# An attention-plus-maxout kernel on one core: subs of eight chunks, the linear term in one phase, evictions over several banks, a fixed order

## The chip, the cores and the metric

The kernel runs on one core of a Trainium2 chip. The metric is the device time of one launch in microseconds, the median of three runs. TensorE (PE in the profile) multiplies and writes to PSUM, which has eight banks of 128 partitions by 512 float32 columns. ScalarE (ACT) and VectorE (DVE) read PSUM and write to SBUF; this is called an eviction here. GpSimd (POOL) and SyncE (SP) mostly issue transfers.

## The reference, cut to what matters

`x` is 4 batches of 12,544 tokens of 128 numbers. Per batch, 32 inducing vectors attend over the tokens and give `h` (32 x 128); each token then attends over `h`. The 50,176 results go through a layer that takes the greater of two products of width 1,024, and a last product back to 128.

```python
def mab(q, kv):                       # softmax attention, scale = 1/sqrt(128)
    s = scale * (q @ kv.transpose(0, 2, 1))
    a = np.exp(s - s.max(-1, keepdims=True))
    a /= a.sum(-1, keepdims=True) + 1e-09
    return a @ kv
h = mab(inducing, x)                  # per batch: 32 x 128
y = mab(x, h).reshape(50176, 128)
g = np.maximum(y @ w1, y @ w2)        # 50176 x 1024
out = g @ w_out                       # 50176 x 128
```

Before and after use `max(a, b) = a + relu(b - a)`. With `e` the 32 exponentials of a token, `b - a` is `e @ hwd` with `hwd = h (w2 - w1)`, and `a @ w_out` is `e @ m1` with `m1 = h w1 w_out`. So a token's output is `(relu(e @ hwd) @ w_out + e @ m1) / sum(e)`. The second term is the **linear term**.

## The kernel before

A chunk is 128 tokens; a batch has 98 chunks, and there are 392. Because `e` has 32 rows, four products `e @ hwd` can run at once, each in its own 32 rows of TensorE's array (row tiles). The kernel therefore has four quarters `q`, each with its own chunks. A **stage** computes `e` of up to 16 chunks in four column tiles (128 x 32) and takes the exponential on ScalarE. A **phase** is a run of row-tile matmuls (32 x 128): each quarter fills one PSUM bank of 512 columns, which ScalarE or VectorE evicts with a relu.

```python
for i in range(4):                       # phase(): the four quarters side by side
    for seq in parts_:
        if i < len(seq):
            nc.tensor.matmul(**seq[i])   # 1 of 512 columns, or 2 of 256, or 4 of 128
...
if max(ck.act, ready) + 0.477 <= max(ck.dve, ready) + 0.597:
    nc.scalar.activation(out=dst, in_=src, func=AF.Relu)      # one bank
else:
    nc.vector.tensor_scalar(out=dst, in0=src, scalar1=0.0, scalar2=None, op0=ALU.max)
```

A **final** is one full-array matmul (128 x 128, 128 columns) that multiplies the relu of one chunk and one eighth of the width by `w_out`; a chunk has eight, so there are 3,136. Finals add up in the bank of their group, which is up to four chunks of one quarter. That bank was opened by the linear term of the group, which took the place of one quarter's unit in a phase; a few groups at the ends take the linear term with full-array matmuls instead.

```python
if kind == "L":                          # a group's linear term in place of a unit
    for s, (_, t) in enumerate(a.chunks):
        seq.append(dict(out=ps[:, 128 * s : 128 * (s + 1)],
                        lhsT=a.blk.e2[r, 128 * t : 128 * (t + 1)],
                        rhs=st[qu.b]["m1"][r, :], start=(s == 0), stop=False, ...))
...
nc.tensor.matmul(                        # final_one()
    out=g.ps[:, 128 * c : 128 * (c + 1)],
    lhsT=g.blk.relu[q][:, 128 * (jb * w4 + t) : 128 * (jb * w4 + t + 1)],
    rhs=woutp[:, jb, :], start=(g.full and state["mm"] == 0), ...)
...
nc.vector.tensor_mul(osb[:, 0:n, :], g.ps[...], rp)   # evict_group(): times 1 / sum(e)
nc.sync.dma_start(out=outr[b, :, c : c + m, :], in_=osb[:, s : s + m, :])
```

What comes next is chosen while the program is built. A class `Clock` keeps an estimate of when each engine and bank is free, and a loop takes a phase, a final, a stage or a part of the next batch's first attention. Where the estimate shows TensorE without work, `keep_busy` puts in matmuls of zeros.

```python
while state["g"] < len(groups) or held:
    side_work()
    ...
    if tp < INF and lag() <= 128 + LIMIT and (tp <= ck.pe + early or tp <= tf and tf > ck.pe):
        phase(jobs)
    elif tf < INF:
        keep_busy(tf)
        final_one()
```

The next batch's attention over its tokens (L309 to L370 in the profile: scores, transposes by DMA, sums in column tiles) is interleaved with the current batch's phases and finals.

Of the kernel before, what the change touches and what calls it, by code (L numbers as in the profile page):

```python
# [16 lines left out]
INF = 1e9  # L17

# [42 lines left out]
class Quarter:  # L61


    def __init__(self, b, c0, w):
        self.b, self.c0, self.w = b, c0, w
        self.subs = {1: [1], 2: [2], 3: [2, 1], 4: [4]}[w]


class Block:


    def __init__(self, quarters, full=()):
        self.quarters = quarters
        self.width = max(qu.w for qu in quarters if qu)
        self.b = [qu.b for qu in quarters if qu][0]
        self.staged = None
        self.rp = None
        self.units = []
        self.done = {}
        self.relu = {}  # L80
        self.last_group = {}
        self.groups = []
        for q, qu in enumerate(quarters):
            jobs = []
            t0 = 0
            for w in qu.subs if qu else []:
                for u in range(2 * w):
                    jobs.append((q, t0, w, u))
                t0 += w
            self.units.append(jobs)  # L90
            if qu:
                self.groups.append(Group(self, [(q, t) for t in range(qu.w)], q in full))


class Group:
    def __init__(self, blk, chunks, full):
        self.blk, self.chunks, self.full = blk, chunks, full
        self.q = chunks[0][0]
        self.bank = self.ps = None
# [3 lines left out]
def kernel(  # L103
# [17 lines left out]
    P1 = 14  # L121
    DOWN = 2.0**-14
    NE2 = 5
    WARM = 9
# [16 lines left out]

    def bank(shape, dtype=F32, only=None):
        i = min(range(8), key=lambda j: ck.bank[j]) if only is None else only
        uid[0] += 1
        return i, psum.tile(shape, dtype, name=f"ps{uid[0]}", tag=f"bank{i}", bufs=1)
# [38 lines left out]
    w2h = relup.tile([128, 4096], F16, name="w2h", tag="relu0")[:, 0:J]  # L184
    w1h = relup.tile([128, 4096], F16, name="w1h", tag="relu1")[:, 0:J]
# [5 lines left out]
    m1bd = consts.tile([128, 4, C], F16, name="m1bd")  # L191
# [5 lines left out]
    with tc.manual_schedule(engines={ET.PE, ET.DVE, ET.Activation, ET.Pool, ET.SP}):  # L197

        xf = relup.tile([128, 4096], F16, name="xf", tag="relu2")[:, 0 : 256 * P1].bitcast(F32)
# [17 lines left out]
        for q in range(4):  # L217
            nc.vector.memset(ones_q[32 * q : 32 * (q + 1), q : q + 1], 1.0)
        nc.gpsimd.memset(m1bd, 0.0)
# [216 lines left out]
        def small_sums(es, ready):  # L436

            ps = st[0]["eps"]
            ck.wait(ready, "p1")
            nc.tensor.matmul(out=ps[:, 2:3], lhsT=rep32, rhs=es, start=True, stop=True, skip_group_check=True)  # L440
            end = ck.run(0.11)
            st[0]["rs"] = smp.tile([128, 1], F32, name="rs_0", tag="rs_")
            st[0]["rw"] = smp.tile([128, 1], F32, name="rw_0", tag="rw_")
            nc.vector.reciprocal(out=st[0]["rs"], in_=ps[:, 2:3])
            nc.vector.tensor_scalar(out=st[0]["rw"], in0=st[0]["rs"], scalar1=1.0 / scale, scalar2=None, op0=ALU.mult)
            ck.bank[st[0]["eb"]] = st[0]["rsr"] = ck.on_dve(end, 0.34)

        def small_hwd(b, halves=(0, 1)):
            if 0 in halves:
                st[b]["hwd"] = smp.tile([128, J], F16, name=f"hwd_{b}", tag="hwd")  # L450
            hwd = st[b]["hwd"]
            for half in halves:
                for n in range(2 if b == 0 and half == 0 else 1):
                    w = 256 if b == 0 and half == 0 else 512
                    bi, ps = bank([128, 512])
                    ps = ps[:, 0:w]
                    sl = slice(512 * half + w * n, 512 * half + w * (n + 1))
                    ck.wait(max(ck.bank[bi], st[b]["hT4r"]), "p1")
                    if b == 0:
                        nc.tensor.matmul(out=ps, lhsT=st[b]["hT4"], rhs=w2h[:, sl], start=True, stop=False)  # L460
                        nc.tensor.matmul(out=ps, lhsT=st[b]["hT4"], rhs=w1h[:, sl], start=False, stop=True)
                        end = ck.run(0.43 * w / 512)
                    else:
                        nc.tensor.matmul(out=ps, lhsT=st[b]["hT4"], rhs=w21[:, sl], start=True, stop=True)  # L464
                        end = ck.run(0.215)
                    if half == 0 and n == 0:
                        if b == 0:
                            nc.vector.tensor_scalar(
                                out=hwd[:, sl], in0=ps, scalar1=st[0]["rw"], scalar2=None, op0=ALU.mult
                            )  # L470
                        else:
                            nc.vector.tensor_copy(out=hwd[:, sl], in_=ps)
                        ck.bank[bi] = ck.on_dve(end, 0.07 + w / 970.0)
                    else:
                        nc.scalar.activation(
                            out=hwd[:, sl], in_=ps, func=AF.Copy, scale=st[0]["rw"] if b == 0 else 1.0
                        )
                        ck.bank[bi] = ck.on_act(end, 0.06 + w / 1200.0)
                    st[b]["hwdr"] = max(ck.bank[bi], st[b].get("hwdr", 0.0))

        def small_m1(b):
# [5 lines left out]
            bd = {0: [0], B - 1: [0, 1, 2, 3]}.get(b, [])  # L487
            outs = [(m1bd[32 * q : 32 * (q + 1), q, :], slice(32 * q, 32 * (q + 1))) for q in bd]
            for o, r in outs + [(m1, slice(0, 128))]:
                if b == 0:  # L490
                    nc.vector.tensor_scalar(
                        out=o, in0=ps[r, 0:128], scalar1=st[0]["rw"][r, :], scalar2=None, op0=ALU.mult
                    )
                else:
                    nc.vector.tensor_copy(out=o, in_=ps[r, 0:128])
                ck.bank[bi] = ck.on_dve(end, 0.2)
# [18 lines left out]
        def weights_2():  # L515
            for g in range(2):
                bi, ps = bank([128, 4, 128], F16)
                ck.wait(ck.bank[bi], "w")
                for j in range(4):
                    jb = 4 * g + j  # L520
                    nc.tensor.transpose(ps[:, j, :], w1h[:, 128 * jb : 128 * (jb + 1)], identity16)
                end = ck.run(0.056 * 4)
                if g == 0:
                    nc.vector.tensor_copy(out=w1T[:, 0:4, :], in_=ps)
                    ck.bank[bi] = ck.on_dve(end, 0.4)
                else:
                    nc.scalar.copy(out=w1T[:, 4:8, :], in_=ps)
                    ck.bank[bi] = w_of["w1T"] = ck.on_act(end, 0.5)

        def weights_3():  # L530
# [15 lines left out]
        def shapes(b):  # L546

            four = [(4, 4, 4, 4)]
            if b == 0:
                return [(1, 2, 3, 4)] + four * 5 + [(2, 2, 2, 2)]  # L550
            if b == 1:
                return four * 6 + [(1, 1, 0, 0)]
            if b == 2:
                return four * 6 + [(0, 0, 1, 1)]
            return four * 5 + [(2, 2, 2, 2), (4, 3, 2, 1)]

        blocks = []
        for b in range(B):
            c0 = 0
            for shape in shapes(b):  # L560
                quarters = []
                for w in shape:
                    quarters.append(Quarter(b, c0, w) if w else None)
                    c0 += w
                blocks.append(Block(quarters, (0,) if not blocks else (0, 1, 2, 3) if shape == (4, 3, 2, 1) else ()))
            assert c0 == K

        def stage(blk):
            bi, ps = bank([128, 512])
            wd = blk.width  # L570
            some = [qu for qu in blk.quarters if qu]
            ck.wait(max(ck.bank[bi], st[some[0].b]["hT4r"]), "stage bank")
            for q in range(4):
                qu = blk.quarters[q] or some[0]
                hq = st[qu.b]["hT4"][:, 32 * q : 32 * (q + 1)]
                xT = xT_tiles[qu.b % 2]
                lo = qu.c0 if qu.c0 + wd <= K else K - wd
                pieces = [(0, qu.c0, min(wd, K - qu.c0))]
                if pieces[0][2] < wd:
                    pieces.append((pieces[0][2], lo, wd - pieces[0][2]))  # L580
                for t, c, n in pieces:
                    nc.tensor.matmul(  # L582
                        out=ps[32 * q : 32 * (q + 1), 128 * t : 128 * (t + n)],
                        lhsT=hq,
# [576 lines left out]
```

The softmax here doesn't subtract the row's maximum and nothing guards it: scores larger than these inputs give would overflow.

## Time and profile before

| | before |
|---|---|
| median of 3 runs | 330.41 us (330.19 to 330.61) |
| span of the profiled execution | 328.5 us |
| busy: TensorE, VectorE, ScalarE | 98%, 87%, 85% of the span |
| mean granted TensorE clock | 1.00 |
| finals (L792), row-tile matmuls of phases (L957) | 3,136 and 1,261 |
| relu evictions: ScalarE (L973), VectorE (L976) | 463 and 321, one bank each |
| evictions of results (L819) | 108 |

Matmuls overlap in the pipeline, so the busy time of a TensorE line counts a stretch once even if several are in flight, and the mean of one (220 ns for a final) is a latency and not what it adds to the time. What one adds is the distance from start to start. For ScalarE and VectorE the mean also overlaps a little with the next instruction. "x" is a count; idle time is that of the engine just before the group, with what ended most of it.

### The profile page before, as it was taken

What the parts mean: (1) busy time and instruction counts of PE and PEld (TensorE: products, weight loads), DVE (VectorE), ACT (ScalarE), POOL (GpSimd) and SP (SyncE); (2) the same over time, 40 slices, a digit from 0 to 9 for tenths busy, and PEclk for the clock granted to TensorE, in tenths of its full rate; (3) what the DMA queues carried; (4) which work ended last, traced back from release to release, by engine and by line L of the source; (5) the groups of instructions that cost most, each with busy time, mean ns of one, the idle gap of its engine ahead of it and who ended that gap; (6) DMA issues with size and microseconds to landing.
All of it is one profiled execution on the core that took longest, in us unless ns stands there. A gap on an engine that the chain in (4) does not pass through costs nothing.

```text
span 328.5 us, 12601 instructions
## 1 busy us (share of the span) xinstructions
PE 322.6 (98%) x5401; PEld 244.1 (74%) x5401; DVE 285.3 (87%) x532; ACT 280.7 (85%) x562; POOL 25.7 (8%) x54
## 2 busy tenths in 40 slices
PE   8999999999999999999999999999999999999996
PEld 3876777777777777777777777777777777778785
DVE  3359899999988999998989989988989989989873
ACT  3679899998789999988888999998968999999961
POOL 7351030000310000000040000000000000000000
PEclk9999999999999999999999999999999999999999
DMA  8999999964299999672479999983212312222233
GB/s 207 208 206 213 289 237 205 216 187 124 57 227 244 229 221 213 167 155 97 132 139 245 226 257 215 197 177 100 98 66 97 114 67 99 98 98 98 80 116 114
DMA packets 70823, 53.65 MB, mean 163 GB/s; under 512 B 52176, under 2 KB 55408, under 8 KB 70768
## 3 DMA queue, kind: packets, MB, share of 16 engines
q1 hardware_dynamic: 64656, 38.63, 47.4%
q0 software_dynamic: 6112, 14.22, 22.1%
q8 instruction: 42, 0.69, 0.9%
q14 instruction: 13, 0.11, 0.1%
HBM read 28.33 MB, written 25.69 MB: 164 GB/s over the span
## 4 chain that ended last, share of the span: by engine, by line
PE 96%; DVE 1%; issue 1%; ACT 0%; DVEq 0%; ACTq 0%
PE ps L792 60%; PE ps L957 22%; PE ps L582 3%; PE ps L232 2%; PE ps L357 1%; PE ps L309 1%; PE ps L648 1%; PE ps L248 1%; PE ps L280 1%; PE ps L622 1%; DVE relu L976 1%; PE ps L749 1%; PE ps L271 1%; PE ps L640 0%; PE ps L464 0%
## 5 line engine op out<-in xcount | busy, mean ns | idle before, releaser
L973 ACT ACTIVATE relu<-ps 128x512 f16<-128x512 f32 x463 | 244.6, 604 | 31.1 <-PE ps L957 24.1
L976 DVE TENSOR_SCALAR relu<-ps 128x512 f16<-128x512 f32 x321 | 205.8, 681 | 18.8 <-PE ps L957 17.9
L792 PE MATMUL ps<-woutp,relu 128*128 128x128 f16 x3136 | 218.1, 220 | 0.0
L792 PEld LDWEIGHTS <-relu 128*128 128x128 f16 x3136 | 177.3, 98 | 39.4 <-issue 28.3
L957 PE MATMUL ps<-e,hwd 32*128 32x512 f16 (+2 forms) x880 | 89.0, 360 | 0.0
L819 DVE TENSOR_TENSOR o<-ps,rp 128x512 f32<-128x512 f32 (+3 forms) x108 | 68.6, 635 | 5.7 <-PE ps L792 3.1
L957 PEld LDWEIGHTS <-hwd 32*128 32x128 f16 x880 | 25.0, 91 | 21.1 <-issue 0.8
L957 PE MATMUL ps<-m,e 32*128 32x128 f16 x381 | 38.8, 217 | 0.0
L957 PEld LDWEIGHTS <-e 32*128 32x128 f16 x381 | 21.4, 92 | 2.6
L165 POOL DMA_DIRECT2D xn<-in_x_dram x31 | 16.7, 551 | 8.4 <-DMA xn<-in_x_dram 4.4
L236 DVE COPY xT<-ps 128x512 f16<-128x512 f16 (+3 forms) x11 | 5.5, 504 | 8.1 <-PE ps L232 8.0
L594 ACT ACTIVATE e<-ps 128x512 f16<-128x512 f32 (+2 forms) x21 | 11.6, 572 | 0.0
L320 ACT ACTIVATE eu<-ps 128x512 f16<-128x512 f32 x18 | 10.8, 619 | 0.0
L582 PE MATMUL ps<-xT,hT 128*32 128x512 f16 (+3 forms) x114 | 10.4, 366 | 0.0
L164 POOL COPY pace<-esr 128x1 f32<-128x1 f32 x2 | 0.4, 183 | 116.6 <-DVE esr L391 116.6
L239 ACT COPY xT<-ps 128x768 f16<-128x768 f16 (+3 forms) x11 | 6.1, 557 | 3.0 <-PE ps L232 2.9
L232 PE MATMUL ps<-identity,xn 128*128 128x128 f16 x98 | 7.7, 224 | 0.1
L582 PEld LDWEIGHTS <-hT 128*32 128x32 f16 x114 | 2.9, 93 | 5.9 <-issue 5.2
L232 PEld LDWEIGHTS <-xn 128*128 128x128 f16 x98 | 5.9, 100 | 1.3 <-DVE xn L644 0.9
L257 ACT ACTIVATE et<-ps 128x448 f16<-128x448 f32 (+4 forms) x11 | 4.5, 413 | 2.6 <-PE ps L248 2.6
L632 DVE RECIPROCAL rp<-ps 128x16 f32<-128x16 f32 (+2 forms) x28 | 6.7, 239 | 0.0
L622 PE MATMUL ps<-ones_q,e 128*128 128x4 f16 x102 | 6.5, 165 | 0.0
(96 smaller groups left out, 117.5 us busy)
## 6 DMA issues: line engine op xcount, KB each, us to landing
out_dram<-o SPq DMA_DIRECT2D x90, 256.0 KB, 2.5
xn<-in_x_dram POOLq DMA_DIRECT2D x24, 448.0 KB, 11.9
out_dram<-o SPq DMA_DIRECT2D x10, 128.0 KB, 3.1
xn<-in_moe_w_dram POOLq DMA_DIRECT2D x4, 256.0 KB, 14.1
xn<-in_x_dram POOLq DMA_DIRECT2D x4, 224.0 KB, 10.2
xT<-xn SPq DMA_TRANSPOSE x42, 3.8
xf<-in_x_dram SPq DMA_DIRECT2D x1, 512.0 KB, 3.7
xf<-in_x_dram SPq DMA_DIRECT2D x1, 384.0 KB, 4.1
```

What stands on the lines that cost most here:

```text
L165: nc.gpsimd.dma_start(out=xn_at[b, i][:, 0:n, :], in_=xr[b, :, k0 : k0 + n, :])
L232: nc.tensor.transpose(ps[:, j, :], xn[:, g + j, :], identity16)
L320: nc.scalar.activation(out=eu, in_=ps, func=AF.Exp, scale=scale, accum_out=st[b]["es"][:, u : u + 1])
L582: nc.tensor.matmul(out=ps[32 * q : 32 * (q + 1), 128 * t : 128 * (t + n)], lhsT=hq, rhs=xT[:, c : c + n, :], start=True, stop=True, tile_p ...
L594: nc.scalar.activation(out=blk.e2[:, 0 : 128 * wd], in_=ps[:, 0 : 128 * wd], func=AF.Exp, scale=st[0]["rs"] if blk.b == 0 else scale,)
L622: nc.tensor.matmul(out=ps[:, 4 * t : 4 * t + 4], lhsT=blk.e2[:, 128 * t : 128 * (t + 1)], rhs=ones_q, start=True, stop=True,)
L632: nc.vector.reciprocal(out=blk.rp[:, 0:wd, :].rearrange("p t q -> p (t q)"), in_=ps[:, 0 : 4 * wd])
L792: nc.tensor.matmul(out=g.ps[:, 128 * c : 128 * (c + 1)], lhsT=g.blk.relu[q][:, 128 * (jb * w4 + t) : 128 * (jb * w4 + t + 1)], rhs=woutp[: ...
L819: nc.vector.tensor_mul(osb[:, 0:n, :], g.ps[:, 0 : n * C].rearrange("p (s c) -> p s c", s=n), rp)
L957: nc.tensor.matmul(**seq[i])
L973: nc.scalar.activation(out=dst, in_=src, func=AF.Relu)
L976: nc.vector.tensor_scalar(out=dst, in0=src, scalar1=0.0, scalar2=None, op0=ALU.max)
```

## The change

A **sub** is now eight chunks in token order, two for each quarter, and there are 49. Every sub has exactly four phases; in each, every quarter makes two eighths of the width for its two chunks, as two matmuls of 256 columns. Quarters 0 and 2 belong to result bank `a`, quarters 1 and 3 to bank `b`, and each of these two banks takes four chunks and 32 finals. The linear term of all eight chunks of a sub rides in one phase of a later sub, as two further matmuls of 128 columns per quarter. Two quarters then write to the same result bank from different row tiles. Quarters 0 and 1 do their linear part first and quarters 2 and 3 last, and a semaphore makes the latter wait until the former have been written.

All of PSUM is one tile, so one relu instruction can read two or three adjacent banks. Which engine evicts which banks, which banks are used, and the order of everything in the main part stand in a list, `ORDER`, that is part of the source; the loop, its readiness rules and `keep_busy` are gone. In that list `PA2D1A1:426L` is a phase whose banks start at 4, 2 and 6: ScalarE takes two, VectorE one, ScalarE one, and the L adds a linear term; `a8` and `b6` are finals.

The aims are phases that are all alike and fewer in number, fewer instructions on the evicting engines, and an order that was fixed beforehand.

```diff
-        def phase(jobs):
-            free = sorted(range(8), key=lambda j: ck.bank[j])
...
-                if kind == "L":
-                    qu = a.blk.quarters[q]
-                    for s, (_, t) in enumerate(a.chunks):
...
-            for i in range(4):
-                for seq in parts_:
-                    if i < len(seq):
-                        nc.tensor.matmul(**seq[i])
+        def phase(segs, banks, linear):
...
+            for i, (q, b) in enumerate(zip((0, 2, 1, 3), units)):
+                seqs[q] = [
+                    dict(
+                        out=ps_all[:, b, 256 * jj : 256 * (jj + 1)],
+                        lhsT=st[sub.at[q][0]]["hwd"][r, 128 * (2 * p + jj) : 128 * (2 * p + jj + 1)],
+                        rhs=sub.tile.e2[r, 256 * sub.slot : 256 * (sub.slot + 1)],
...
+                    for jj in range(2)
+                ]
+            if linear:
...
+                ln = linear_of(ls)
+                for q in range(4):
+                    seqs[q] = ln[q] + seqs[q] if q < 2 else seqs[q] + ln[q]
+            for i in range(len(seqs[0])):
+                for q, seq in enumerate(seqs):
+                    if linear and (i, q) == (2, 2):
+
+                        nc.tensor.wait_ge(apart, at["linear"])
+                    nc.tensor.matmul(**seq[i])
+                    if linear and (i, q) == (1, 1):
+                        at["linear"] += 1
+                        nc.tensor.drain(fusable=True).then_inc(apart, 1)
...
+                dst = sub.relu.rearrange("p (i x) -> p i x", i=4)[:, i : i + w, 512 * p : 512 * (p + 1)]
+                src = ps_all[:, b : b + w, :]
+                if e == "A":
                     nc.scalar.activation(out=dst, in_=src, func=AF.Relu)
                 else:
                     nc.vector.tensor_scalar(out=dst, in0=src, scalar1=0.0, scalar2=None, op0=ALU.max)
...
-        while state["g"] < len(groups) or held:
-            side_work()
...
-                keep_busy(tf)
...
+        run(ORDER)
```

In the built program the drain is no instruction of its own: the matmul of quarter 1 raises the semaphore when it is done, and the weight load of quarter 2's first linear matmul waits for it. Smaller parts of the change: the full-array linear matmuls and their block-diagonal `m1bd` are gone, the weights' transposes go through one bank and one VectorE copy, and the staging buffers follow the subs.

## Prediction

> **What bounds the kernel now.** I read the page's busy shares first, then the chain that ended last, then the costliest groups:
>
> ```profile
> PE 322.6 (98%) x5401; PEld 244.1 (74%) x5401; DVE 285.3 (87%) x532; ACT 280.7 (85%) x562; POOL 25.7 (8%) x54
> ...
> PE 96%; DVE 1%; issue 1%; ACT 0%; DVEq 0%; ACTq 0%
> ...
> L973 ACT ACTIVATE relu<-ps 128x512 f16<-128x512 f32 x463 | 244.6, 604 | 31.1 <-PE ps L957 24.1
> L976 DVE TENSOR_SCALAR relu<-ps 128x512 f16<-128x512 f32 x321 | 205.8, 681 | 18.8 <-PE ps L957 17.9
> L792 PE MATMUL ps<-woutp,relu 128*128 128x128 f16 x3136 | 218.1, 220 | 0.0
> ```
>
> TensorE has work in 98% of the span and holds 96% of the chain. The evicting engines' idle time ends mostly with a matmul of L957: they wait for TensorE, not TensorE for them. So the time is the sum of what TensorE does, and I need the price of each piece. The chain in order of time gives it (start, length, line; two stretches of it):
>
> ```profile
> 45.61 0.33 PE ps L957 x4
> 45.94 0.89 PE ps L792 x14
> 46.82 0.33 PE ps L957 x4
> 47.15 0.89 PE ps L792 x14
> ```
>
> ```profile
> 314.35 0.33 PE ps L957 x4
> 314.68 2.34 PE ps L792 x40
> 317.02 0.34 PE ps L957 x6
> 317.36 0.55 PE ps L792 x8
> ```
>
> From the second stretch, a final costs (2.34 - 0.55) / 32 = 0.056 us, and 0.55 - 8 x 0.056 = 0.10 us is left over: the change from full array to row tiles. A final streams 128 columns, so a phase of 512 columns streams for 4 x 0.056 = 0.22 us; it takes 0.33, so the change back costs another 0.11. A phase thus costs 0.33 + 0.11 = 0.44 us, half of it mode changes. A phase with six matmuls takes 0.34, so shape hardly counts.
>
> Over the whole trace I sorted the matmuls by tile mode: 487 changes with a median of 0.108 us more than the streaming, 53 us in all. Between 30.5 and 325 us all but 7.7 us is streaming and changes, and about 2.6 of the 7.7 are the float32 matmuls that normalise `h`. There is little waiting to be won.
>
> **What the Trainium skill says.** "TensorEngine Tiling (Array Packing)", Tiling Modes, Key Properties: changing the tiling mode drains TensorE, changing the tile within a mode doesn't. The trace agrees: 0.10 to 0.11 us at each change. The same page, Gotcha 1: PSUM Pressure: different row tiles can't access one PSUM bank at the same time, and software must see to it. That is what the new semaphore is for; the kernel before gives each quarter its own bank, so its trace doesn't show it. "Perfetto Trace Analysis", Tensor Engine Instruction: a matmul's semaphore goes out once PSUM has acknowledged all bytes, after the end that the profile estimates. The trace shows how much later, in a window at 205 us (start, length, work; the idle time stands in brackets):
>
> ```profile
> 205.17 0.39 PE L957 MATMUL ps<-e,hwd 32*128 32x512 f16 x4
> ...
> 205.59 0.60 ACT L973 ACTIVATE relu<-ps 128x512 f16<-128x512 f32 x1 [0.31 <-PE ps L957]
> ```
>
> ScalarE was idle and began 0.43 us after the phase began. In most such places it is 0.42. Less 0.22 of streaming, the matmul's end reaches another engine 0.20 us after its last column.
>
> **The change part by part.**
>
> Finals: 3,136 before and after, the same 175 us of streaming. The relu products cover the same 784 bank-fuls.
>
> Phases: the order of the two programs has 222 runs of row-tile matmuls before and 195 after (49 x 4, two of them adjacent). Linear terms no longer take a quarter's turn. 27 runs fewer, at 0.44 us: **-11.9 us**. Mode changes fall from 487 to 433, exactly two for each such run; column-tile runs (38) stay.
>
> Linear terms: 49 phases stream 256 columns more per quarter, 2 x 0.056 = 0.11 us: **+5.4 us**.
>
> The new wait, in a linear phase counted from its start: quarters 0 and 1 stream two linear matmuls until 0.11. At 0.11 + 0.20 = 0.31 the semaphore is seen. Quarters 2 and 3 have streamed their two 256-column matmuls by 0.22 and could go on then. So 0.09 us is lost, and the weight load behind the wait, which otherwise hides, may show too (92 ns for one load of L957). I take 0.13, between 0.09 and 0.18; nothing else can fill it, as TensorE goes in order. 49 x 0.13: **+6.4 us**. This is the term I trust least.
>
> Fills and full-array linear terms: 13 matmuls of 256 zero columns (0.11 each) and 11 of 128 columns go: **-2.0 us**.
>
> The doubled count of row-tile matmuls (1,261 to 1,960) I give no cost: phases of 256- or 128-column pieces take 0.33 to 0.34 us in the trace of before.
>
> Evictions: beside TensorE, so only their capacity counts. Consecutive relus start 0.50 us apart on ScalarE (three span 1.61: (1.61 - 0.60) / 2) and 0.61 apart on VectorE (two span 1.29: 1.29 - 0.68). A second bank adds only streaming: on ScalarE (799 - 479) / 384 = 0.83 ns per column from the copies of 768 and 384, so 0.43 us; on VectorE (684 - 418) / 256 = 1.04 ns from L819, so 0.53 us. The list has 308 single, 94 double and one triple on ScalarE (499 banks), 265 single and 10 double on VectorE (285). ScalarE: 308 x 0.50 + 94 x 0.93 + 1.4 = 243 us against 463 x 0.50 = 232, so **11 us more**. VectorE: 265 x 0.61 + 10 x 1.14 = 173 against 196, so **23 us less**, with 98 result evictions for 108. ScalarE would be near 89% busy and VectorE near 79%: neither is the bound on the whole.
>
> The end: before, the last eviction has 128 columns and takes 0.29 us; after, it has 512, 0.68 us: **+0.4 us**. The last transfer grows from 64 to 256 KB; the issue table shows no longer landing for larger ones (4.5 and 2.5 us).
>
> Start and waits: the fills before stand between 26 and 29.7 us, where TensorE had little to do; the list puts the weights' transposes and products there. Against that, new waits can come. I put **-0.6 us** for both, an estimate, not a measurement.
>
> Sum: 330.4 - 11.9 + 5.4 + 6.4 - 2.0 + 0.4 - 0.6 = 328.1. I say **328.0 us**.
>
> **The rivals.**
>
> *The linear wait is free or dear.* If TensorE sees its own semaphore at once, all 6.4 us come back: 321.7. If the wait empties the array as a mode change does and the weight load follows in the open, it may cost 0.25 us: 334. For the first: a semaphore that needn't cross engines could be quicker. For the second: all eviction starts in the trace show 0.20 us.
>
> *ScalarE or the banks become the bound.* Adding up the list's first 28 phases, ScalarE has 38.6 us of work against 40.5 us on TensorE; later stretches have 81 to 92%. A double eviction holds two banks for about a microsecond, and two banks belong to results, so six remain for phases that need four at a time. The kernel before also runs ScalarE at 35.23 of 37 us between 23 and 60 us without holding up TensorE, which speaks against it. If 60 phases waited 0.1 us each: +6, 334.
>
> *The fixed order removes the rest of the waits.* About 5 us of waiting between 30 and 325 us isn't float32 work. A better order could win 3 to 4: 324. The order before was already close to its floor, so more isn't there.
>
> **Range and chances.** Step 1 of the sum (-11.9 + 5.4 - 2.0) is nearly a count, good to 1 us. The wait can move it by -6 to +6, bank waits by up to +6, the order by -4; these are partly independent. I take **322.0 to 334.0** for 8 in 10. Faster by over 2% means below 323.8, which needs a free wait or a much better order: **0.17**. Slower by over 2% means above 337.0, two rivals at once: **0.06**. Within 2%: **0.77**.
>
> **What would show each step.** Runs of row-tile matmuls: plain phases still at 0.33 us in the chain; linear ones at 0.33 + 0.11 + 0.13 = 0.57; were they at 0.44, the wait is free. ScalarE's mean for a two-bank relu near 1.03 us (604 + 427 ns) and VectorE's near 1.21. TensorE still near 98% busy and most of the chain; ScalarE's idle time still ended by TensorE. If TensorE's phases wait for ScalarE's relu in sum over 5 us, the second rival holds. Fills gone near 26 us, and the first 16 finals done no later than before. The prediction is wrong if 256-column phases cost more than 0.33 us each, since there are 147 of them without a linear term and 0.02 us each is 3 us.

## The result and the profile after

The changed kernel takes **342.2 us** (median of four runs, 341.28 to 342.84) against 330.3 us (330.17 to 330.61) before, measured on the same chip: a ratio of 1.036, with a 95% interval of 1.033 to 1.038. It is slower by 11.9 us, where the prediction had it 2.4 us faster, at 328.0 us (322.0 to 334.0). The profiled spans are 328.5 and 340.4 us and differ by the same 11.9 us.

First the page of the changed kernel: busy time and share of the span, the chain by engine, and the three costliest groups with busy time, mean ns of one, and idle time with its releaser.

```profile
PE 327.1 (96%) x6066; PEld 241.1 (71%) x6066; DVE 268.1 (79%) x470; ACT 290.2 (85%) x499; POOL 25.5 (8%) x54
...
PE 87%; DVE 5%; DMA 4%; ACT 2%; issue 1%; SPq 0%; DVEq 0%; ACTq 0%
...
L855 ACT ACTIVATE relu<-ps_all 128x512 f16<-128x512 f32 (+1 forms) x403 | 251.9, 706 | 25.8 <-PE ps_all L844 22.1
L791 PE MATMUL ps_all<-woutp,relu 128*128 128x128 f16 x3136 | 214.9, 220 | 0.6 <-ACT relu L855 0.4
L857 DVE TENSOR_SCALAR relu<-ps_all 128x512 f16<-128x512 f32 (+1 forms) x275 | 185.6, 706 | 35.1 <-PE ps_all L844 30.0
```

TensorE's share of the chain has fallen from 96% to 87%; VectorE, DMAs and ScalarE have taken the rest. No evicting engine is full: ScalarE has 85%, as before. Something has come between engines that all have room.

To see where the 11.9 us are, I sorted the matmuls of both traces by tile mode, as the prediction did for the kernel before: 0.056 us for every 128 columns streamed, 0.108 us for every change of mode. What is left between 30 us and the last matmul is the "rest". Such sums are good to about half a microsecond, since short matmuls can be counted in more than one way.

| | before | after | difference | predicted |
|---|---|---|---|---|
| streaming | 254.1 | 252.4 | -1.7 | -2.6 |
| mode changes (489 and 435 in the traces) | 52.8 | 47.0 | -5.8 | -5.8 |
| rest, inside the linear phases | | 8.2 | +8.2 | +6.4 |
| rest, elsewhere | 7.5 | 17.4 | +9.9 | -0.6, with the start |
| start | | | about +0.4 | |
| last matmul to the end | 3.25 | 4.2 | +0.95 | +0.4 |

What was counted came true to within 1 us. The linear phases cost somewhat more than predicted. The failure is the 9.9 us of waits elsewhere. Three readings of the trace show what these parts are.

**The linear phase.** The timeline of TensorE around 52 us (start, length, work, in groups of matmuls of one kind; lengths include the pipeline's latency, so starts are what to compare):

```profile
52.04 0.23 PE L844 MATMUL ps_all<-m,e 32*128 32x128 f16 x2
...
52.11 0.22 PE L844 MATMUL ps_all<-m,e 32*128 32x128 f16 x2
...
52.41 0.23 PE L844 MATMUL ps_all<-m,e 32*128 32x128 f16 x2
52.42 0.28 PE L844 MATMUL ps_all<-e,hwd 32*128 32x256 f16 x2
...
52.63 0.95 PE L791 MATMUL ps_all<-woutp,relu 128*128 128x128 f16 x14
53.52 0.40 PE L844 MATMUL ps_all<-e,hwd 32*128 32x256 f16 x8
53.85 0.84 PE L791 MATMUL ps_all<-woutp,relu 128*128 128x128 f16 x12
```

The last line but one and the last are a plain phase: 53.85 - 53.52 = 0.33 us. The linear phase takes 52.63 - 52.04 = 0.59 us. In it the second linear matmuls of quarters 0 and 1 begin at 52.11 and have streamed by 52.17; quarters 2 and 3 begin theirs at 52.41, after the semaphore. From the last column to the next matmul it took 0.24 us.

**The short waits.** The waits of the changed kernel (engine and line, what it waited for: us in total, times, longest):

```profile
PEld L844 <- PE ps_all L844: 10.3, 49, 0.2
...
PE ps_all L844 <- DVE relu L857: 3.7, 10, 0.5
...
ACT eu L371 <- DMA eT<-eu: 3.1, 1, 3.1
...
PE ps_all L844 <- ACT eu L371: 2.0, 1, 2.0
```

The first line is the semaphore, 49 times 0.21 us of an idle weight loader; the phases grow by less, 0.15 to 0.17 us each. The second was not foreseen. The timeline around 107 us shows one of the ten (idle time before the instruction and its releaser in brackets):

```profile
106.48 0.69 DVE L765 TENSOR_TENSOR o<-ps_all,rp 128x512 f32<-128x512 f32 x1 [0.87 <-PE ps_all L844]
107.09 0.68 DVE L857 TENSOR_SCALAR relu<-ps_all 128x512 f16<-128x512 f32 x1
...
107.20 0.28 PE L844 MATMUL ps_all<-e,hwd 32*128 32x256 f16 x3
...
107.83 0.37 PE L844 MATMUL ps_all<-e,hwd 32*128 32x256 f16 x5 [0.34 <-DVE relu L857]
...
108.13 1.01 PE L791 MATMUL ps_all<-woutp,relu 128*128 128x128 f16 x15
```

VectorE had been idle for 0.87 us. Then the linear phase released two pieces of work at once: the eviction of a result (`o`), which `close` issues, and a relu. In the queue the result stands first, so the relu begins 0.61 us later than it could. The next phase wants the relu's bank and stops after three matmuls. VectorE is 79% busy and still late. From start to start this phase takes 108.13 - 107.20 = 0.93 us and not 0.33: it loses 0.60 us, of which the row of waits counts 0.34, because a matmul that has streamed still shows as busy for the rest of its length.

**The long wait.** Two views of the same moment, ScalarE's timeline and TensorE's:

```profile
67.60 0.22 ACT L391 ACTIVATE et<-ps_all 128x64 f16<-128x64 f32 x1
70.91 0.60 ACT L371 ACTIVATE eu<-ps_all 128x512 f16<-128x512 f32 x1 [3.09 <-DMA eT<-eu]
```

```profile
69.36 0.29 PE L844 MATMUL ps_all<-e,hwd 32*128 32x256 f16 x3
71.65 0.37 PE L844 MATMUL ps_all<-e,hwd 32*128 32x256 f16 x5 [2.00 <-ACT eu L371]
...
73.65 1.67 PE L791 MATMUL ps_all<-woutp,relu 128*128 128x128 f16 x14
```

The exponentials `eu` of the next batch's attention have a ring of five buffers. The sixth must wait until the first has been read by its transposing DMA, which started at 66.02 and ran until 70.81. Meanwhile the sixth scores stay in their PSUM bank. The list has `s1:4 PD1A1A1D1:1265 b14 PD1A1A2:713`: the scores go to bank 4, and the second phase behind them needs banks 7, 1, 3 and 4. It stops after three matmuls, and TensorE stands still for 2.0 us. Four relus stand behind the exponential in ScalarE's queue and come late too. In the kernel before, the sixth scores began 3.6 us after the first transpose (69.82 and 66.25), which had landed by then; in the list they begin 1.8 us after it (67.81 and 66.02), and this transpose took 4.8 us, against 3.0 before and a median of 2.5 for the 18 of this trace. Both orders are fixed before the launch; the loop of the kernel before only left more room. The last line shows that it doesn't end there: 14 finals take 1.6 us from 73.72 in the chain, where they take 0.89 elsewhere. The windows (length, busy time and count of TensorE, weight loads, VectorE, ScalarE and GpSimd, granted clock, DMA share, GB/s) show why; first those of the kernel before, then those of the changed one:

```profile
core 0: us, PE busy (x) PEld busy (x) DVE busy (x) ACT busy (x) POOL busy (x), PEclk, DMA share, GB/s
...
68.00:72.00 4.00, 4.00 (x67) 2.78 (x64) 3.82 (x7) 4.00 (x11) 0.00 (x0) 1.00 0.55 135
72.00:76.00 4.00, 4.00 (x94) 3.18 (x92) 3.68 (x8) 4.00 (x9) 0.00 (x0) 1.00 0.49 135
```

```profile
68.00:72.00 4.00, 2.00 (x35) 1.17 (x32) 1.96 (x5) 1.09 (x4) 0.00 (x0) 1.00 1.26 120
72.00:76.00 4.00, 4.00 (x54) 2.79 (x53) 2.58 (x5) 2.95 (x6) 0.00 (x0) 0.63 0.60 164
```

After the standstill the granted clock was 0.63 in the mean from 72 to 76 us (the trace's record of the clock has 1.0 until 73.05, 0.5 until 76.46, then 1.0), with 54 matmuls where 108 follow in the 4 us after. The Trainium skill, "TensorE: Matmul & The Clock Gate", Part 1, says that the clock is halved when TensorE has been idle for about a window of 3.4 us. The trace agrees in kind, and differs in size: 2.0 us of standstill were enough. Length alone does not settle it, as two of the runs below show: after 1.72 us in e7 the clock stayed at 1.00, after 1.60 us in e10 (178.56 to 180.16) it was 0.57 from 181 to 185 us.

### The profile page after: what moved, and what is told of

It reads as the page before. It is cut to its first block, busy times and chain, and to the rows that moved or that the text cites. A ratio compares the mean times of both kernels' runs of the same rounds, so it can differ in the third digit from the quotient of the medians.

```text
span 340.4 us, 14033 instructions
## 1 busy us (share of the span) xinstructions
PE 327.1 (96%) x6066; PEld 241.1 (71%) x6066; DVE 268.1 (79%) x470; ACT 290.2 (85%) x499; POOL 25.5 (8%) x54
## 4 chain that ended last, share of the span: by engine, by line
PE 87%; DVE 5%; DMA 4%; ACT 2%; issue 1%; SPq 0%; DVEq 0%; ACTq 0%
PE ps_all L791 53%; PE ps_all L844 23%; DVE o L765 2%; PE ps_all L615 2%; DVE relu L857 2%; PE ps_all L283 2%; PE ps_all L408 2%; DMA eT<-eu 1%; PE ps_all L360 1%; DMA early<-in_x_dram 1%; DMA xT<-xn 1%; ACT relu L855 1%; PE ps_all L299 1%; PE ps_all L331 1%; PE ps_all L646 1%
## 5 line engine op out<-in xcount | busy, mean ns | idle before, releaser
L855 ACT ACTIVATE relu<-ps_all 128x512 f16<-128x512 f32 (+1 forms) x403 | 251.9, 706 | 25.8 <-PE ps_all L844 22.1
L791 PE MATMUL ps_all<-woutp,relu 128*128 128x128 f16 x3136 | 214.9, 220 | 0.6 <-ACT relu L855 0.4
L857 DVE TENSOR_SCALAR relu<-ps_all 128x512 f16<-128x512 f32 (+1 forms) x275 | 185.6, 706 | 35.1 <-PE ps_all L844 30.0
L844 PE MATMUL ps_all<-e,hwd 32*128 32x256 f16 x1568 | 96.7, 273 | 6.1 <-DVE relu L857 3.7
L765 DVE TENSOR_TENSOR o<-ps_all,rp 128x512 f32<-128x512 f32 x98 | 66.9, 683 | 14.8 <-PE ps_all L844 11.1
L844 PEld LDWEIGHTS <-hwd 32*128 32x128 f16 x1568 | 33.8, 92 | 26.5 <-issue 12.5
L844 PE MATMUL ps_all<-m,e 32*128 32x128 f16 x392 | 28.6, 221 | 0.0
L844 PEld LDWEIGHTS <-e 32*128 32x128 f16 x392 | 11.9, 92 | 15.9 <-PE ps_all L844 10.3
L371 ACT ACTIVATE eu<-ps_all 128x512 f16<-128x512 f32 x18 | 10.8, 598 | 7.1 <-PE ps_all L360 3.6
L635 ACT ACTIVATE e<-ps_all 128x512 f16<-128x512 f32 x18 | 10.1, 603 | 0.5 <-PE ps_all L615 0.5
## 6 DMA issues: line engine op xcount, KB each, us to landing
xn<-in_x_dram POOLq DMA_DIRECT2D x24, 448.0 KB, 11.9
```

The source lines that it names most:

```text
L371: nc.scalar.activation(out=eu, in_=ps, func=AF.Exp, scale=scale, accum_out=st[b]["es"][:, u : u + 1])
L635: nc.scalar.activation(out=tl.e2[:, 256 * lo : 256 * hi], in_=ps[:, 256 * lo : 256 * hi], func=AF.Exp, scale=f)
L765: nc.vector.tensor_mul(osb, sub.ps[a].rearrange("p (s c) -> p s c", s=4), sub.tile.rp[:, lo : lo + 4, None].broadcast_to((128, 4, C)),)
L791: nc.tensor.matmul(out=sub.ps[a][:, 128 * i : 128 * (i + 1)], lhsT=sub.relu[:, lo : lo + 128], rhs=woutp[:, jb, :], start=not sub.begun[a] ...
```

## The experiments

The theory: the 9.9 us are the two kinds of waits above, made by the order of queues and not by a lack of capacity; and the linear phases' 8.2 us are the semaphore. The rivals are these: the evictions over two banks hold banks too long; the weight load behind the semaphore's wait, not the semaphore's way, is what costs; the program is simply at the limit of its banks. Ratios are to the kernel before, with 95% intervals; "us" are medians.

**e1_eu6: a sixth buffer for the exponentials.**

```diff
-            eu = etp.tile([128, 512], F16, name=f"eu_{b}_{u}", tag="eu", bufs=NEU)
+            eu = etp.tile([128, 512], F16, name=f"eu_{b}_{u}", tag="eu", bufs=NEU + 1)
```

> The changed kernel (342.2 us) with six instead of five buffers for the exponentials eu of the next batch's attention; nothing else. Theory: the one stall at 69 to 76 us begins with ScalarE, which stands 3.1 us before its sixth eu until the transposing DMA has read the first; the matmul of a phase then waits 2.0 us for ScalarE, and TensorE's granted clock falls to 0.63 in the next 4 us. Without that wait the clock stays at 1.0 and the stretch from 60 to 100 us loses what it has more than before beyond streaming and mode changes, 7.0 - 1.9 = 5.1 us: about 337 us, 336 to 338.5. Rival: the transposes by DMA are late in any case, and the wait moves to the sums that need them (L408): above 340.5 us with a new wait for a DMA.

Measured: 338.61 us (338.25 to 339.01), ratio 1.025 (1.024 to 1.027): 3.6 us less, a little less of a gain than expected. The same windows now:

```profile
68.00:72.00 4.00, 4.00 (x77) 2.90 (x77) 3.98 (x8) 3.73 (x8) 0.00 (x0) 1.00 0.82 102
72.00:76.00 4.00, 4.00 (x115) 2.94 (x107) 3.19 (x8) 3.42 (x6) 0.00 (x0) 1.00 0.59 130
```

TensorE is busy throughout, the clock is full, and 192 matmuls stand where there were 89. One wait of 2.0 us cost 3.6: the 3.41 us at half the clock, from 73.05 to 76.46, account for up to 1.7 us more. The ten short waits are untouched (3.6 us).

**e2_olast: the result's eviction behind the relus of its phase.**

```diff
-            if linear:
-                close(ls)
             i = 0
             for (e, w), b in zip(segs, banks):
...
                 i += w
+            if linear:
+                close(ls)
```

> The changed kernel with one change of order on VectorE: in a phase with a linear term, the eviction of the result bank (0.69 us) comes after the relu evictions of that phase and not ahead of them. Theory: the ten waits of a phase for VectorE's relu (3.7 us directly, some 0.6 us each with what follows) come from the result eviction that stands in front of a relu whose bank the next phase needs. They go, and the time falls by 4 to 6 us to 336 to 338.5; the result bank comes free 0.6 us later, which should cost less than 1 us. Rival: the banks are short because a double eviction holds two of them; then the order of VectorE's queue changes little, and the time stays at 341 to 343 us with the waits in place.

Measured: 335.18 us (333.38 to 335.6), ratio 1.013 (1.010 to 1.016): 7.0 us less. No phase waits for VectorE's relu any more, and the long wait stays (2.0 us on TensorE, 3.1 on ScalarE). The gain is more than the 3.7 us that the row named and more than expected, because the row counts idle time only, and of ten waits. From start to start, 17 phases and runs of finals in the changed trace lose 0.2 to 0.6 us each that they do not lose here, 7.6 us in all.

**e3_nowait: no semaphore.** Quarters 2 and 3 write their linear matmuls into their own phase bank, where the phase then overwrites them. The matmuls and their columns stay, and no two quarters write to one bank any more. The output lacks half of the linear term.

```diff
-                    seqs[q] = ln[q] + seqs[q] if q < 2 else seqs[q] + ln[q]
+                    if q > 1:
+                        for t in (0, 1):
+                            ln[q][t]["out"] = ps_all[:, units[(0, 2, 1, 3).index(q)], 128 * t : 128 * (t + 1)]
+                            ln[q][t]["start"] = True
+                    seqs[q] = ln[q] + seqs[q]
...
-                    if linear and (i, q) == (2, 2):
-
-                        nc.tensor.wait_ge(apart, at["linear"])
                     nc.tensor.matmul(**seq[i])
-                    if linear and (i, q) == (1, 1):
-                        at["linear"] += 1
-                        nc.tensor.drain(fusable=True).then_inc(apart, 1)
```

> The changed kernel without the semaphore in the linear phases: quarters 2 and 3 make their two linear matmuls first, into their own phase bank, where the relu products then overwrite them. So the linear term of half of the chunks is left out of the output, while the count of matmuls, the streaming and the mode changes stay. Theory: a linear phase falls from 0.59 to 0.33 + 0.11 = 0.44 us, 49 x 0.15 = 7.5 us less: 334.5 us, 333 to 336.5. Rival: the extra time of a linear phase comes from sixteen small matmuls with weight loads and not from the semaphore: a linear phase stays above 0.5 us and the time above 338 us.

Measured: 331.27 us (330.41 to 333.93), ratio 1.004 (1.003 to 1.006): 10.9 us less. The linear phase fell from 0.592 to 0.442 us, 0.15 x 49 = 7.4 us. The other 3.5 us came with it: the waits for VectorE's relu fell from ten of up to 0.5 us to two of 0.3, ScalarE's wait for the DMA from 3.1 to 2.0, and TensorE's behind it from 2.0 to 0.9. Its runs spread over 3.5 us, and the profiled one had half the clock from 23.0 to 29.8 us, which the changed kernel's had not. So this run can't give the semaphore's price alone; e12 below comes closer.

**e4_single: each eviction of ScalarE over several banks as single ones.**

```diff
-                    nc.scalar.activation(out=dst, in_=src, func=AF.Relu)
+                    for k in range(w):
+                        nc.scalar.activation(out=dst[:, k, :], in_=src[:, k, :], func=AF.Relu)
```

> The changed kernel with every eviction of two or three banks on ScalarE done as single ones on the same banks in the same order (96 instructions more on ScalarE). Theory: the double evictions are no cause of the loss; they save ScalarE a little under 0.1 us each, so without them ScalarE has 7 to 9 us more work, part of it in front of phases: 342 to 347 us. Rival: two banks held for a microsecond are what the phases wait for; single evictions free the first one 0.5 us sooner, and the time falls by 3 us or more, below 339 us.

Measured: 343.39 us (341.63 to 344.68), ratio 1.039 (1.035 to 1.043): 1.2 us more than the changed kernel. The ten waits for VectorE's relu are there as before (3.7 us), so it was not the double evictions that made them. The rival that they hold the banks too long falls. The 1.2 us are no price, though: in this profile TensorE waited only 0.6 us for the sixth exponential instead of 2.0, and the clock stayed at 1.00 there. e11 gives the price.

**e5_both: e1 and e2 together.**

> Both repairs of the changed kernel together: six buffers eu, and VectorE's result evictions behind the relus. Alone the first gave 3.6 us (338.6) and the second 7.0 us (335.2). Theory of two independent causes: the gains add up, 342.2 - 3.6 - 7.0 = 331.6 us, 330.8 to 333; no phase waits 0.3 us or more for ScalarE or VectorE, and the granted clock is at 1.00. Rival: the second run had won a part of the same time (its stall at 70 us was also shorter), and the sum stays at 333.5 us or above.

Measured: 331.27 us (330.81 to 332.11), ratio 1.003 (1.001 to 1.004). The gains add up, 3.6 + 7.0 = 10.6 against 10.9 measured. Of the four waits shown above, one is left:

```profile
PEld L844 <- PE ps_all L844: 10.2, 49, 0.2
```

The rest between 30 us and the last matmul is 14.5 us, 7.9 of it in linear phases. That closes the account: counted parts -7.5, rest 14.5 - 7.5 = +7.0, start and end +1.35, together +0.9, and the medians differ by 331.27 - 330.35 = 0.9 us. The two waits are the loss that the prediction lacked; the design without them is 0.3% slower than the kernel before. So a shortage of banks was not what cost the 11.9 us.

**e6_mmwait: the wait on the matmul instead of on the weight load before it.** If part of the 0.15 us is a weight load of 92 ns that comes only after the wait, it should go.

```diff
+                    mm = nc.tensor.matmul(**seq[i])
                     if linear and (i, q) == (2, 2):
-
-                        nc.tensor.wait_ge(apart, at["linear"])
-                    nc.tensor.matmul(**seq[i])
+                        mm._wait_ge(apart, at["linear"])
```

> The changed kernel with the wait for the semaphore moved from the weight load to the linear matmul of quarter 2, so that the weights are loaded while it waits; nothing else. Theory: of the 0.15 us that a linear phase takes beyond its streaming, 0.09 is the way of the semaphore, and the rest is the weight load behind it; a linear phase falls from 0.59 to 0.53 to 0.56 us and the time by 1.5 to 3 us to 339 to 340.7. Rival: TensorE doesn't load weights of the row tile ahead, or the semaphore's way is all of it: 0.58 us or more and 341.5 us or more.

Measured: 342.59 us (342.11 to 343.14), ratio 1.037 (1.035 to 1.039), linear phase 0.589 us. No gain: the weight load costs nothing here, and the semaphore's way is nearly the whole of the wait.

**e7_all: e1, e2 and e6 together.**

> The three repairs together: six buffers eu, result evictions behind the relus, the wait on the matmul. If they add up, 331.6 less 1.5 to 3: 328.6 to 330.2 us, level with the kernel before or up to 0.5% faster. What remains slower than before is then the rest of the wait (about 0.09 x 49 = 4.4 us) and the end (0.9 us); what is faster is 54 mode changes fewer (5.8 us) and 1.7 us less of streaming. Rival: the repairs bring out other waits, since TensorE then asks for banks sooner: 331 us or more.

Measured: 331.24 us (330.68 to 334.15), ratio 1.004 (1.002 to 1.007): the same as e5: the further gain that was expected rested on e6's, which did not come. The runs spread more, and the one profiled took 333.14 us. Its timeline shows a wait that the fixed list can also produce, for the DMA that transposes the next batch's tokens:

```profile
61.41 0.38 PE L360 MATMUL ps_all<-xT,inducingT 128*32 128x512 f16 x1 [1.72 <-DMA xT<-xn]
```

**e8_best: e7, the relu products of quarters 0 and 1 drawn ahead of the wait, and the last result in two halves on two queues.**

```diff
+            turn = [(i, q) for i in range(len(seqs[0])) for q in range(4)]
+            if linear:
+                turn[8:] = [(2, 0), (2, 1), (3, 0), (3, 1), (2, 2), (2, 3), (3, 2), (3, 3)]
...
+            if sub.n == NS - 1 and a == 1:
+                for h, eng in ((0, nc.sync), (2, nc.scalar)):
+                    nc.vector.tensor_mul(osb[:, h : h + 2, :], ...)
+                    eng.dma_start(out=outr[b, :, c + h : c + h + 2, :], in_=osb[:, h : h + 2, :])
```

> The three repairs, and two more: in a linear phase quarters 0 and 1 finish their relu products before the wait and not behind it, so that their evictions start some 0.1 us sooner; and the last result bank is evicted in two halves with two transfers on two queues. Theory: the first changes the length of the phase by under 0.02 us but shortens the remaining waits for evictions a little (0 to 1 us), the second shortens the end by 0.2 to 0.5 us: 0.3 to 1.5 us below the run with the three repairs, so 327.5 to 330. Rival: neither is on the path: the same as that run within 0.3 us.

Measured: 330.92 us (330.11 to 334.46), ratio 1.003 (1.001 to 1.005). The linear phase stays at 0.584 us, and from the last matmul to the end it is 4.28 us: neither edit shows in the time. The phase still ends with the linear columns of quarters 2 and 3, which can't begin before the semaphore, and a transfer of half the size ends no earlier.

**e9_later: e8, with one group of scores (the entry `s1:7`) behind the next phase in the list,** so that the DMA of e7's line has more time.

```diff
-a17 b4:0 s1:7 PA1D1D1A1:4153L a8 b8
+a17 b4:0 PA1D1D1A1:4153L s1:7 a8 b8
```

> The run before with five edits (330.9 us, single runs from 330.1 to 334.5) with one entry of the list moved: the fourth batch-1 scores (s1) come after the next phase and not ahead of it. Theory: its single runs spread because this matmul sometimes reads chunks whose transposing DMA has not landed; in the profile of the run with three repairs TensorE stood there 2.1 us (waiting for the DMA of xT), in the one with five edits 0.3 us. With 0.6 to 0.9 us more time the wait goes or shrinks: median 329.7 to 330.7 us and fewer single runs above 332. Rival: the spread comes from elsewhere: median and spread stay.

Measured: 331.12 us (330.63 to 332.88), ratio 1.003 (1.002 to 1.004). The spread is narrower (2.3 us for 4.4), the median the same.

**e10_split: the linear term over two phases.** The semaphore's way would lie beneath the finals between two phases. In 45 of 49 subs, quarters 0 and 1 do their linear part at the end of one phase and quarters 2 and 3 at the end of the next; the wait stands in the second. The result that opened this bank is evicted after the second phase. It stands on e9, without e6 and without e8's new order within the phase.

```diff
+                    if q < 2:
+                        seqs[q] = ln[q] + seqs[q] if whole else seqs[q] + ln[q]
+                    elif whole:
+                        seqs[q] = seqs[q] + ln[q]
...
+            elif ls is not None:
+                for q in (2, 3):
+                    seqs[q] = seqs[q] + ls.rest[q]
+                ls.linear = True
...
-            if linear:
+            if ls is not None and ls.linear:
                 close(ls)
```

> Six buffers eu, result evictions behind the relus, the end in two halves, the fourth scores later, and the linear term of 45 of the 49 subs split over two phases: quarters 0 and 1 in the phase of the list, quarters 2 and 3 in the next one, each after their relu products. Nothing has to wait within a phase, as the finals lie between. Theory: such a pair of phases takes 2 x (0.33 + 0.11) = 0.88 us where 0.33 + 0.59 = 0.92 was needed, 45 x 0.04 = 1.8 us less; the result bank comes free one phase later, which may cost some of it: 328 to 330 us, faster than the kernel before by up to 0.6%. Rival: the later result eviction (1.4 us) makes phases wait for banks: 331 us or more.

Measured: 364.87 us (364.55 to 365.76), ratio 1.104 (1.103 to 1.105). The phases take 0.441 us, as computed, so the semaphore is hidden. But among the waits stand now:

```profile
PE ps_all L885 <- DVE o L781: 9.2, 17, 1.1
PE ps_all L808 <- DVE o L781: 8.7, 10, 1.4
```

Phases (L885) and finals (L808) wait for the eviction of results, and so do the scores and products of the attention, 2.4 to 3.5 us each in three further lines. The list gives the result's bank to the next user right after the one phase in which it is closed; one phase later is too late. In this list the banks have no slack, and 33.6 us are lost against e5.

**e11_single_rep: e5 with single evictions,** as in e4, now that no other wait hides what they do.

> The kernel with two repairs (six buffers eu, result evictions behind the relus; 331.3 us) with every double or triple eviction on ScalarE done as single ones. Theory: with the other waits gone, the 0.1 us that a double eviction saves on ScalarE is mostly hidden behind TensorE; 96 instructions more, some 8 us of ScalarE's time, cost 0.5 to 3 us: 331.8 to 334.3. Rival 1: double evictions are worth nothing: 331.3 within 0.4 us. Rival 2: they hold banks too long: below 330.8 us.

Measured: 333.31 us (332.78 to 333.45), ratio 1.009 (1.007 to 1.011): 2.0 us more than e5. So the evictions over two banks are worth about 2 us to this design. Their own sizes in the changed kernel, grouped by shape:

```profile
L855 ACT ACTIVATE relu<-ps_all 128x512 f16<-128x512 f32 x308 | 167.8, 605 | 16.4 <-PE ps_all L844 13.7 <-ACT relu L855 0.9
L855 ACT ACTIVATE relu<-ps_all 128x1024 f16<-128x1024 f32 x94 | 96.0, 1028 | 9.0 <-PE ps_all L844 8.1 <-ACT eu L371 0.2 <-ACT relu L855 0.2
```

**e12_nowait_rep: e5 without the semaphore,** as in e3; the output lacks half of the linear term.

> The kernel with two repairs (331.3 us) with the linear matmuls of quarters 2 and 3 written into their own phase bank ahead of the relu products and then overwritten, so that no semaphore is needed; half of the linear term is left out of the output, the count of matmuls stays. Theory: 49 x 0.15 = 7.4 us less and nothing else to wait for: 323.9 us, 323 to 325, which is 2% under the kernel before: 27 runs of row-tile matmuls fewer and no fills, less what the linear terms stream. Rival: part of the 10.9 us that the same edit gave without the repairs was the repaired waits, and new waits for evictions appear once TensorE is faster: 326 us or more.

Measured: 325.87 us (325.2 to 327.43), ratio 0.987 (0.985 to 0.990): 5.4 us less than e5. A linear phase in its timeline:

```profile
51.85 0.29 PE L845 MATMUL ps_all<-m,e 32*128 32x128 f16 x8
51.98 0.39 PE L845 MATMUL ps_all<-e,hwd 32*128 32x256 f16 x8
52.30 0.95 PE L791 MATMUL ps_all<-woutp,relu 128*128 128x128 f16 x14
```

From 51.85 to 52.30, 0.45 us; the median of all is 0.442, which is the plain 0.33 and the 0.11 of its own columns. Computed from the medians of the phases 7.4 us should have come back; the time fell by 5.4. In the two traces all linear phases together take 29.9 and 23.2 us, 6.7 less, and the spans differ by 6.3; the rest is within the spread of the runs (325.2 to 327.43 here). Without the two waits and the semaphore, this design would be 1.3% faster than before.

No version with the whole computation beat the kernel before: the best has 330.92 against 330.35 us. Leaving out the wait alone, with two quarters still writing into one bank, was not tried, so no run here shows what would come of it; nor was a list made anew with two banks for each pair of quarters.

## Why the prediction was wrong

**The counted step held.** 27 row-tile runs fewer, 49 linear loads more and the fills gone were put at -8.5 us together; streaming and mode changes fell by 7.5. The plain phase with 256-column pieces takes 0.33 us (the median of 145), so doubling the matmuls cost nothing, as said.

**The new wait was nearly right.** Linear phases were to take 0.57 us and take 0.592. The mis-sized number is the semaphore's way: ScalarE began 0.20 us after a matmul's last column, and I took that for TensorE as well, but TensorE sees its own semaphore after 0.24 to 0.25. Nor do all eviction starts show 0.20: VectorE's relus in the trace of before began 0.22 to 0.23 us after it in the median. The weight load, which I added as a possible extra, is not part of it (e6). By the phases the term is 7.4 to 8.2 us instead of 6.4. Neither form of the first rival came: it is not free (321.7), and not 0.25 us a phase (334).

**"Start and waits, -0.6 us" is the step that failed.** It was the only term without a count, and it was about +10 (9.9 of waits and 0.4 at the start). e1 and e2 show what it hid: 3.6 us for one ring of five buffers, 7.0 us for results standing before relus. That both waits would come could have been read beforehand: the source has `close(ls)` before the loop of evictions, and the list shows where the sixth group of scores stands against the first transposing DMA. How long the second would be could not: the first transpose took 4.8 us here and 3.0 in the trace of before. I compared the work and the capacity of ScalarE over 28 phases, and this says nothing of the order in one queue.

**The second rival came nearer in size and missed the cause.** It allowed +6 us for 60 waits of 0.1 us at ScalarE and the banks. What came were fewer and longer waits for VectorE's relus and one of 2.0 us for an exponential, on engines with 21% and 15% of their time free. TensorE waited for ScalarE's relus 0.4 us in all, and two-bank evictions were no part of the loss (e4, e11). A two-bank relu of ScalarE takes 1028 ns (1.03 us predicted), and ScalarE's share is 85% (89% predicted).

**The third rival fell,** and its reverse was true: the new order was to win 3 to 4 us and lost about 10. The prediction did say that new waits can come, but set them against a gain at the start and gave them no size.

**The end** cost 0.95 us instead of 0.4: 4.2 us from the last matmul for 3.25. About half of it is the longer eviction, as computed: it ends 0.82 us after the last matmul, against 0.33 before. The other half comes after it: 3.4 us to the end, against 2.9. Halving the last transfer left these 3.4 us as they were (e8), so its size alone is not the cause; what is stays open.

**The range** was too narrow for what it left out. With the two waits repaired, the kernel takes 331.3 us, inside it. The 3.2 us still above the sum of 328.1 are the wait (7.9 - 6.4 = +1.5), the counted part (+1.0) and the end (+0.55); once repaired, start and other waits come to 14.5 - 7.9 - 7.5 + 0.4 = -0.5, close to the -0.6 of the sum.

## What to carry to other kernels

Before a share of busy time is taken to show that an engine has room, look at the order in its queue wherever one phase releases two instructions at once: the one that the next phase waits for should stand first (7.0 us here). For each ring of buffers in a fixed order, ask what the engine does if the transfer that frees the buffer comes late; all that stands behind it in the queue waits too, and so does the PSUM bank that it was to empty. A term of a sum without a count is not zero: give it the width of the largest wait that the new order could make.

## What the runs showed of the hardware

TensorE saw the semaphore of its own matmul 0.24 to 0.25 us after the last column, later than ScalarE saw one in the trace of before (0.20 us). Whether that wait stood on a weight load or on the matmul behind it made no difference beyond the noise (342.2 and 342.59 us, linear phases of 0.592 and 0.589 us).

A standstill of 2.0 us was followed by a mean granted clock of 0.63 from 72 to 76 us, so that one wait on TensorE cost 3.6 us of time. A standstill of 1.72 us in another run was not followed by a lower clock.
